# Moving the softmax normalization of attention rows from the writer to the reader: sparse attention and capacity routing on one core

## The chip, the cores and the metric

The kernel runs on one core of one Trainium2 chip. The metric is device time in microseconds (us) of one execution. Before the change, three runs took 1037.57, 1035.76 and 1036.93 us, a median of 1036.93 us. One more execution was recorded by the hardware profiler; its own time was 1035.21 us, and the span from its first to its last instruction is 1033.4 us.

Engines go by the names of the profile: PE multiplies matrices, PEld loads its weights, DVE is the vector engine, ACT the scalar engine, POOL the general-purpose engine (GpSimd), SP issues DMAs. Each engine takes its instructions in the order in which the program lists them.

## The reference

All data are 32-bit floats. Attention runs over 8 batches, 8 heads, 576 positions, 64 elements per head. Its output rows (4608 tokens of 512 elements) go into a mixture of 8 experts in which each expert takes exactly 576 tokens.

```
scores = q @ k^T / 8
scores below (row maximum - tau) are dropped
attn   = exp(scores - max) / sum(exp(scores - max))
x      = attn @ v, the 8 heads of a token side by side   # 4608 x 512
logits = x @ w_gate                                      # 4608 x 8
pairs (token, expert) are taken from the largest logit down;
   an expert that has 576 tokens is full
out[token] = relu(x[token] @ w1[e]) @ w2[e]              # 512 -> 1024 -> 512
```

The division by the sum is a factor for each token and head, so a token of 512 elements has eight factors. It can be applied at any point between `attn @ v` and the expert's first matrix product.

## The kernel before

**Attention.** Four pairs of heads per batch, nine score tiles per pair. PE makes scores, DVE takes the row minimum of the negated scores (`mx`, L74) and applies the threshold (`stt`, L89), ACT takes the exponential (L85), POOL adds tau to the row's extreme (L75), PE transposes the probabilities (L98) and multiplies them by v (L144). The result lies transposed (elements on partitions) and unnormalized in `XT`, one tile per batch. DVE computes reciprocals of the sums into `RD[b]` (token-major, nine columns per pair) and `RD["m",b]` (for the last 64 tokens of a batch).

**Rows.** `xt_unit(b,c)` (L197) turns one chunk of a batch's `XT` back to rows: four PE transposes (L201) into a PSUM bank, then a read of that bank, then a DMA on SP's queue to `xrows` in DRAM (L215). There are five chunks a batch: four of 128 tokens and one of 64 (c = 4), so 40 in all. Two PSUM banks alternate (`bank_v`). For batches 0 and 1 these units run among the attention work, and DVE multiplies by the factors as it reads PSUM (L208, into tile `xr`). For batches 2 to 7 they are kept in `late`; batches 2 and 3 lie in DRAM meanwhile (`xts`). These 30 late units run after the last score tile. There ACT copies PSUM to SBUF and POOL multiplies by the factors (L214, into a free `pp` tile), except for c = 4, where ACT does both in eight pieces of 64 elements (L212).

**Search.** `Router.phase` finds the first expert's tokens: a threshold search of seven levels. A level is a DVE comparison of all best logits with 16 or 32 candidates (`step_cmp`), counts on PE (L403), a DVE copy, flags through PE (L409) and DVE, a broadcast through PE (L419, L424), and a DVE step to the next candidates. Then `pick` chooses the expert, and `pack` (L538) builds the list `idx` of its 576 token numbers. The search for the first expert is interleaved with the 30 late units by the loop at L298: a late unit every `XTY` = 1.05 us of a planned clock, search steps at their planned times. DVE instructions of the router go through the wrapper `Vec`, all shown on line L341.

**Experts.** `moe` keeps jobs (generators) on a planned clock. Each job puts its instructions into the engines' queues and yields a planned wait; `ffn` advances the clock with each matrix product, and the jobs that are due are put in between. So the planned waits set the order of the queues, not the times. An expert r passes through: the search (`R.phase`, waits lengthened by `LATS[r]`), `packing`, then `rows` (L609). `rows` gathers the expert's rows with five indirect DMAs on POOL's queue (L615), waits `GA[r]`, and for each of the five tiles has four PE transposes (L625), an ACT rounding into `xh` (L628), a wait of 0.8, a DVE subtraction into `xl` (the rounding's rest), and a wait of `RW[r]` (0.2, 0.6, 1.0, then 2.0). Two weight jobs split `w1` and `w2` the same way (ACT rounds, DVE subtracts). `ffn` of expert r starts in the plan when its weights and rows are marked done: all five row tiles for r of 2 and more; three tiles (c = 4, 0, 1) for r of 0 and 1, which start with one half of the tokens. While it isn't done, the plan's clock runs on without matrix products. For r = 0 and 1, POOL does most of the subtractions behind relu (L655); for r of 2 and more, DVE does them. `place` runs one search after the other; for r = 0 it waits 2.3 after the packing, closes the expert (`R.close`, five DVE instructions that mark taken tokens and the full expert), waits 1.4 and begins the next search.

Of the kernel before, what the change touches and what calls it, by code (L numbers as in the profile page):

```python
# [9 lines left out]
F32 = mybir.dt.float32  # L10
# [3 lines left out]
AF = mybir.ActivationFunctionType  # L14
ALU = mybir.AluOpType
# [3 lines left out]
S=576; D=64; HS=288; QK=3*HS+2*S  # L19
PPB=8; LTB=1; VTB=5; HOLD=1; CAPV=3.3; RATE=(2.4,2.4); NBO=2; XAC=(4,); NDEF=4; XTB=4; XTY=1.05; XT0=2.0; XRB=2  # L20


def attention(ctx, tc, qk, vl, tau, wgd, xrows, xts, Lg, nb_batches, ident, swap, R, after_first):
# [129 lines left out]
    RD={}  # L153
# [43 lines left out]
    def xt_unit(b,c):  # L197
        ps=bank_v([128,4,128])
        n=128 if c<4 else 64
        for j in range(4):  # L200
            T.transpose(ps[:n,j],XT[b][:,j,c*128:c*128+n],ident)  # L201
        if b<nb_batches-NDEF-NBO: xr=wk.tile([128,512],F32,name="xr",bufs=XRB)
        else: xr=wk.tile([128,2,S],F32,name="pp",bufs=PPB)[:,0,:512]
        def ev():
            src=RD[b][:,:,2*c:2*c+2] if c<4 else RD["m",b][0:64]
            src=src.unsqueeze(3).to_broadcast([n,4,2,64])
            xv=xr[:n].rearrange("p (j h d) -> p j h d",j=4,h=2); pv=ps[:n].rearrange("p j (h d) -> p j h d",h=2)
            if b<nb_batches-NDEF-NBO: V.tensor_tensor(xv,pv,src,op=ALU.mult)  # L208
            elif c in XAC:
                for j in range(4):  # L210
                    for h in range(2):
                        A.activation(xv[:,j,h],pv[:,j,h],AF.Copy,scale=RD[b][:n,j,2*c+h:2*c+h+1] if c<4 else RD["m",b][0:64,j,h:h+1])  # L212
            else:
                A.activation(xv,pv,AF.Copy); G.tensor_tensor(xv,xv,src,op=ALU.mult)  # L214
            nc.sync.dma_start(xrows[b*S+c*128:b*S+c*128+n,:],xr[:n])  # L215
        return ev
# [335 lines left out]

LATS=[0.15,0.05,0.4]+[0.6]*5; FIX=(0.125,0.2)
GA=[7.0,5.5,7.5,9.0]; HALF=1; WARM=[20,4,50]
W1Y=5.0; L2O=(0,4,1,2,3); L2Z=1; HFB=3; RW=[0.2,0.6,1.0,2.0]; LOWP=(0,1); LPF=7; LOWT=1.4; PREPW=1; WLY=(1.0,1.0)

def moe(ctx,tc,R,start,xrows,w1,w2,out,ident):
# [51 lines left out]
    def rows(r,s):  # L609
        while r>0 and ("x",r-1) not in done: yield 0.5  # L610
        order=(4,0,1,2,3) if r<=HALF else range(5)
        for t in order:
            n=128 if t<4 else 64
            x=wk.tile([128,D],F32,name="xg",bufs=5); s["xg",t]=x
            G.indirect_dma_start(out=x[:n],out_offset=None,in_=xrows,in_offset=IOA(ap=s["idx"][:n,t:t+1],axis=0))  # L615
        s["ei2"]=wk.tile([128,1],I32,name="ei2",bufs=2); G.tensor_copy(s["ei2"],s["ei"])
        done.add(("g",r))
        yield GA[min(r,3)]
        while r>0 and ("l1",r-1) not in done: yield 0.5
        s["xh"]=wk.tile([128,4,576],F32R,name="xh"); s["xl"]=wk.tile([128,4,576],F32R,name="xl")  # L620
        for t in order:
            n=128 if t<4 else 64
            ps=pt.tile([128,4,128],F32,name="pt")
            held[0]+=0.5
# [3 lines left out]
            A.activation(xv("xh"),pv,AF.Copy)  # L628
            yield 0.8
            V.tensor_tensor(xv("xl"),pv,xv("xh").bitcast(F32),op=ALU.subtract)  # L630
            done.add(("row",r,t))
# [47 lines left out]
    def place():  # L679
        for r in range(8):  # L680
# [17 lines left out]
            if r==0:  # L698
                yield from packing(r,s)
                yield 2.3; R.close(); yield 1.4  # L700
            else:
                if r<7: R.close()
                jobs.append([clk[0],packing(r,s)])
                yield 0.1
# [57 lines left out]
def build(tc, qk, vl, tau, wgd, cst_d, w1, w2, out, off, nb=8):  # L762
    nc=tc.nc
    with ExitStack() as ctx:
        ctx.enter_context(tc.manual_schedule())
        cp=ctx.enter_context(tc.tile_pool(name="cst",bufs=1))
        dr=ctx.enter_context(tc.tile_pool(name="dr",bufs=1,space=bass.MemoryType.DRAM))
        xrows=dr.tile([8*S,512],F32,name="xrows")
        xts=dr.tile([8,128,4,S],F32,name="xts")
# [28 lines left out]
```

## Time and profile before

| what | value |
|---|---|
| median of 3 runs | 1036.93 us (1035.76 to 1037.57) |
| the profiled execution's own time | 1035.21 us |
| its span | 1033.4 us |
| PE busy | 975.2 us (94%) |
| DVE busy | 777.4 us (75%) |
| ACT busy | 640.0 us (62%) |
| POOL busy | 323.1 us (31%) |
| mean granted clock of PE | 0.982 of full speed |

A share of busy time is a mean over stages with different limits, so the stages are to be read one by one. Attention's score tiles run to about 482 us, the late rows and the first search from there to 537 us, and the experts from 537 us to the end. A group line of the profile gives line, engine, operation, the tile written and the tiles read, shape and count, then busy time in us and the mean of one in ns, then the engine's idle time before these instructions and what ended it. A row of the timeline gives start and duration in us, then the instruction, and in brackets the idle time before it and what ended it.

### The profile page before, as it was taken

The page shows a single profiled execution, that of the slowest core. Times are in us where ns is not written, and L with a number is a line of the kernel's source. Part 1 is how long each engine was busy: PE and PEld are TensorE (multiplying, and loading weights), DVE is VectorE, ACT ScalarE, POOL GpSimd, SP SyncE. Part 2 cuts the span into 40 slices and gives each one's busy share as a digit, 9 for nine tenths or more (in the row PEclk, how much of TensorE's full clock was granted, in tenths as well). Part 3 has the DMA queues.
Part 4 walks back from the last instruction along what each step waited for, and adds up shares of the span by engine and source line. Part 5 has one row for each costly group of instructions (what it writes and reads, how often), then busy time and mean ns, then how long its engine had stood idle before and what let it go on. Part 6 is the DMA issues. An engine that isn't in the chain of part 4 may idle for free. (4 is left out here: it accounts for less than half of the span.)

```text
span 1033.4 us, 24027 instructions
## 1 busy us (share of the span) xinstructions
PE 975.2 (94%) x9104; PEld 709.5 (69%) x9104; DVE 777.4 (75%) x2085; ACT 640.0 (62%) x1221; POOL 323.1 (31%) x485
## 2 busy tenths in 40 slices
PE   6999999999999999998658899999999999999996
PEld 3555555555555555555547779788897978889895
DVE  6999999999999999996777677757585676744230
ACT  5898888888888888886644335444352534445340
POOL 2333333333333343331653445312204031231201
PEclk9999999999999999999878999999999999999998
DMA  6322133233433222302453251504325052363101
GB/s 224 106 67 96 65 138 127 95 138 113 153 107 107 96 72 100 108 2 93 158 206 122 82 169 48 197 28 131 130 83 168 14 185 75 125 229 127 41 11 41
DMA packets 35715, 113.03 MB, mean 109 GB/s; under 512 B 4368, under 2 KB 4752, under 8 KB 35088
## 3 DMA queue, kind: packets, MB, share of 16 engines
q1 hardware_dynamic: 28496, 89.47, 24.5%
q0 software_dynamic: 5888, 18.88, 5.8%
q10 hardware_dynamic: 1216, 3.15, 0.9%
q8 instruction: 72, 1.18, 0.5%
q14 instruction: 43, 0.35, 0.1%
HBM read 89.19 MB, written 21.23 MB: 107 GB/s over the span
## 5 line engine op out<-in xcount | busy, mean ns | idle before, releaser
L75 POOL TENSOR_SCALAR nb<-nb,taub 128x1 f32<-128x1 f32 x288 | 146.8, 510 | 296.6 <-DVE z L74 256.1
L74 DVE TENSOR_SCALAR_CACHE_REDUCE z<-sc 128x576 f32<-128x576 f32 x288 | 206.0, 752 | 34.0 <-PE sc L69 32.5
L85 ACT ACTIVATE pp<-z,nb 128x576 f32<-128x576 f32 x256 | 187.3, 772 | 34.3 <-DVE z L74 32.8
L89 DVE SCALAR_TENSOR_TENSOR pp<-z,nb,pp 128x576 f32<-128x576 f32 x256 | 199.9, 813 | 0.3
L665 PE MATMUL pf<-w2h,H 128*128 128x512 f32 x576 | 196.1, 402 | 1.1 <-DVE H L341 1.1
L69 PE MATMUL sc<-qk 64*128 64x288 f32 (+1 forms) x1280 | 181.3, 428 | 6.0 <-DMA qk<-qk_dram 5.7
L144 PE MATMUL xo<-pt,vt 128*64 128x288 f32 x1024 | 151.9, 418 | 0.7 <-ACT xt L151 0.7
L113 ACT ACTIVATE pt<-tb 128x512 f32<-128x512 f32 x256 | 140.0, 593 | 13.8 <-PE tb L98 11.7
L98 PEld LDWEIGHTS tb<-ident,pp 64*128 64x128 f32 x2304 | 85.7, 139 | 72.7 <-ACT pt L113 16.8
L665 PE MATMUL pf<-w2l,H 128*128 128x512 f32 x320 | 128.2, 401 | 0.0
L672 POOL DMA_INDIRECT out_dram<-y,idx x40 | 42.0, 1050 | 266.8 <-ACT y L668 170.0
L665 PEld LDWEIGHTS pf<-w2h,H 128*128 128x128 f32 x576 | 106.4, 189 | 19.9 <-DVE H L341 1.5
L98 PE MATMUL tb<-ident,pp 64*128 64x64 f32 x2304 | 108.8, 230 | 11.4 <-ACT pt L113 6.2
L69 PEld LDWEIGHTS sc<-qk 64*128 64x128 f32 (+1 forms) x1280 | 94.3, 179 | 35.9 <-DVE pp L89 9.2
L645 PE MATMUL pf<-xh,w1h 128*128 128x288 f32 x512 | 113.3, 300 | 1.2 <-ACT xh L628 1.2
L645 PE MATMUL pf<-xh,w1l 128*128 128x288 f32 x512 | 113.6, 300 | 0.0
L645 PE MATMUL pf<-xl,w1h 128*128 128x288 f32 x512 | 112.8, 299 | 0.0
L651 ACT ACTIVATE hf<-pf 128x576 f32<-128x576 f32 x64 | 41.7, 652 | 105.0 <-PE pf L645 94.0
L144 PEld LDWEIGHTS xo<-pt,vt 128*64 128x64 f32 x1024 | 62.5, 136 | 63.6 <-issue 26.5
L668 ACT ACTIVATE y<-pf 128x512 f32<-128x512 f32 x40 | 23.9, 598 | 115.9 <-PE pf L665 105.1
L645 PEld LDWEIGHTS pf<-xh,w1h 128*128 128x128 f32 x512 | 82.8, 189 | 3.8 <-ACT xh L628 1.7
L645 PEld LDWEIGHTS pf<-xl,w1h 128*128 128x128 f32 x512 | 82.4, 189 | 0.2 <-DVE xl L341 0.2
(170 smaller groups left out, 1355.5 us busy)
## 6 DMA issues: line engine op xcount, KB each, us to landing
qk<-qk_dram SPq DMA_DIRECT2D x31, 1008.0 KB, 4.9
w2s<-w_dram SPq DMA_DIRECT2D x32, 512.0 KB, 5.9
w1s<-w_dram SPq DMA_DIRECT2D x28, 512.0 KB, 5.8
vt<-vl_dram SPq DMA_DIRECT2D x32, 320.0 KB, 5.4
xrows<-pp SPq DMA_DIRECT2D x24, 256.0 KB, 2.0
xts<-xt SPq DMA_DIRECT2D x2, 1152.0 KB, 5.3
pt<-xts SPq DMA_DIRECT2D x2, 1152.0 KB, 6.8
xrows<-xr SPq DMA_DIRECT2D x8, 256.0 KB, 2.0
```

What stands on the lines that cost most here:

```text
L69: T.matmul(sc[o,f,:HS], kd["q",h][r,c], kd[k,h][r,:],start=True,stop=True)
L74: V.tensor_scalar(z,SC.pop(t)[:,:,:HS],-0.125,None,op0=ALU.mult,op1=ALU.min,accum_out=nb[:,0:1])
L75: G.tensor_scalar(nb[:,1:2],nb[:,0:1],taub[:,0:1],None,op0=ALU.add)
L85: A.activation(pview(t),ZB[t].rearrange("p a b -> p (a b)"),AF.Exp,bias=NBI[t][:,0:1],scale=-1.0)
L89: V.scalar_tensor_tensor(pv,ZB.pop(t).rearrange("p a b -> p (a b)"),NBI[t][:,1:2],pv,op0=ALU.is_le,op1=ALU.mult,accum_out=den_of(p)[:,p%4, ...
L98: g=slice(64*r,64*r+64); T.transpose(o[:,r],x[g],ident[g,g])
L113: A.activation(PT[p][:,i%2,:,(i//2)*128:(i//2+1)*128].rearrange("p k (r q) -> p r k q",r=2),tb,AF.Copy)
L144: T.matmul(xo[64*h:64*h+64,:HS],v[:,u,64*h:64*h+64],PT[p][:,h,u,q],start=(u==0),stop=False,skip_group_check=True)
L645: T.matmul(ps[:,h,:HS],s[w][:,k,f*128:(f+1)*128],s[x][:,k,h*HS:(h+1)*HS], start=(k==0 and j==0),stop=(k==3 and j==2))
L651: A.activation(hf,ps[:,:,:HS],AF.Relu)
L665: T.matmul(ps[:,0,:],H[:,f,c:c+128],s[w][:,f],start=(f==0 and j==0),stop=e)
L672: G.indirect_dma_start(out=out,out_offset=IOA(ap=s["idx"][:n,t:t+1],axis=0),in_=y[:n],in_offset=None)
```

## The change

Rows go to DRAM unnormalized, with their eight factors beside them: a row of `xrows` has 520 elements (2080 bytes) instead of 512 (2048 bytes). The gathered tiles `xg` have the same width, and DVE multiplies each head's 64 elements by its factor before the transposes, for all 40 tiles.

In `xt_unit`, DVE (batches 0 and 1) and ACT (the rest) only copy PSUM to SBUF; the factors are copied by POOL (batches 0 and 1) or ACT (the rest). POOL's multiplications over 512 elements and ACT's eight-piece multiplications for c = 4 are gone. In `rows`, expert 0's multiplications stand between the tiles' other steps; for later experts all five stand ahead of the first transpose, with a planned wait of `SCY` = 1.2 after each. Three planned quantities change: `LATS[1]` from 0.05 to 0.15, `GA` from 7.0, 5.5, 7.5, 9.0 to 6.0, 6.5, 8.0, 9.0, and the start of the second search, which was 3.7 after expert 0's list and now comes when expert 0's third row tile has been put into the queues.

```diff
-PPB=8; LTB=1; VTB=5; HOLD=1; CAPV=3.3; RATE=(2.4,2.4); NBO=2; XAC=(4,); NDEF=4; ...
+PPB=8; LTB=1; VTB=5; HOLD=1; CAPV=3.3; XW=520; RATE=(2.4,2.4); NBO=2; NDEF=4; ...
...
-        if b<nb_batches-NDEF-NBO: xr=wk.tile([128,512],F32,name="xr",bufs=XRB)
-        else: xr=wk.tile([128,2,S],F32,name="pp",bufs=PPB)[:,0,:512]
+        early=b<nb_batches-NDEF-NBO
+        if early: xr=wk.tile([128,XW],F32,name="xr",bufs=XRB)
+        else: xr=wk.tile([128,2,S],F32,name="pp",bufs=PPB)[:,0,:XW]
         def ev():
             src=RD[b][:,:,2*c:2*c+2] if c<4 else RD["m",b][0:64]
-            src=src.unsqueeze(3).to_broadcast([n,4,2,64])
-            xv=xr[:n].rearrange("p (j h d) -> p j h d",j=4,h=2); pv=ps[:n].rearrange("p j (h d) -> p j h d",h=2)
-            if b<nb_batches-NDEF-NBO: V.tensor_tensor(xv,pv,src,op=ALU.mult)
-            elif c in XAC:
-                for j in range(4):
-                    for h in range(2):
-                        A.activation(xv[:,j,h],pv[:,j,h],AF.Copy,scale=RD[b][:n,j,2*c+h:2*c+h+1] if c<4 else RD["m",b][0:64,j,h:h+1])
+            fv=xr[:n,512:XW].rearrange("p (j h) -> p j h",j=4); xv=xr[:n,:512].rearrange("p (j d) -> p j d",j=4)
+            if early:
+                V.tensor_copy(xv,ps[:n]); G.tensor_scalar(fv,src,1.0,0.0,op0=ALU.mult,op1=ALU.add)
             else:
-                A.activation(xv,pv,AF.Copy); G.tensor_tensor(xv,xv,src,op=ALU.mult)
+                A.activation(xv,ps[:n],AF.Copy); A.activation(fv,src,AF.Copy)
...
-LATS=[0.15,0.05,0.4]+[0.6]*5; FIX=(0.125,0.2)
-GA=[7.0,5.5,7.5,9.0]; HALF=1; WARM=[20,4,50]
+SCY=1.2; LATS=[0.15,0.15,0.4]+[0.6]*5; FIX=(0.125,0.2)
+GA=[6.0,6.5,8.0,9.0]; HALF=1; WARM=[20,4,50]
...
-            x=wk.tile([128,D],F32,name="xg",bufs=5); s["xg",t]=x
+            x=wk.tile([128,XW],F32,name="xg",bufs=5); s["xg",t]=x
...
+        def scale(t):
+            n=128 if t<4 else 64
+            v=s["xg",t][:n,:D].rearrange("p (h d) -> p h d",h=8)
+            V.tensor_tensor(v,v,s["xg",t][:n,D:XW].unsqueeze(2).to_broadcast([n,8,64]),op=ALU.mult)
         yield GA[min(r,3)]
+        if r>0:
+            for t in order: scale(t); yield SCY
         while r>0 and ("l1",r-1) not in done: yield 0.5
...
         for t in order:
             n=128 if t<4 else 64
+            if r==0 and t==order[0]: scale(t)
...
             yield 0.8
+            if r==0 and t!=order[-1]: scale(order[order.index(t)+1])
             V.tensor_tensor(xv("xl"),pv,xv("xh").bitcast(F32),op=ALU.subtract)
...
-                yield 2.3; R.close(); yield 1.4
+                yield 2.3; R.close(); yield 0.1
+                while ("row",0,1) not in done: yield 0.1
...
-        xrows=dr.tile([8*S,512],F32,name="xrows")
+        xrows=dr.tile([8*S,XW],F32,name="xrows")
```

More of the change, by code (lines that the diff above doesn't have):

```diff
@@ L19 @@
 S=576; D=64; HS=288; QK=3*HS+2*S
-PPB=8; LTB=1; VTB=5; HOLD=1; CAPV=3.3; RATE=(2.4,2.4); NBO=2; XAC=(4,); NDEF=4; XTB=4; XTY=1.05; XT0=2.0; XRB=2
+PPB=8; LTB=1; VTB=5; HOLD=1; CAPV=3.3; XW=520; RATE=(2.4,2.4); NBO=2; NDEF=4; XTB=4; XTY=1.05; XT0=2.0; XRB=2
 def attention(ctx, tc, qk, vl, tau, wgd, xrows, xts, Lg, nb_batches, ident, swap, R, after_first):
```

## The prediction

> **What bounds the kernel now.** I read the table of stretches first (columns: stretch and its length, busy us and instruction count of PE, PEld, DVE, ACT and POOL, granted PE clock, DMA share, GB/s):
>
> ```profile
> 300.00:400.00 100.00, 98.88 (x1154) 57.44 (x1154) 94.01 (x271) 87.71 (x163) 35.39 (x70) 1.00 0.27 96
> 491.00:531.00 40.00, 24.14 (x221) 18.93 (x222) 28.32 (x61) 23.89 (x72) 27.60 (x24) 0.79 0.51 178
> 531.00:548.00 17.00, 10.15 (x113) 8.62 (x112) 14.10 (x29) 5.81 (x7) 6.72 (x6) 0.70 0.58 193
> 620.00:680.00 60.00, 59.22 (x458) 50.72 (x456) 43.55 (x103) 24.96 (x50) 26.30 (x26) 1.00 0.32 110
> ```
>
> Attention and the experts are bound by PE (98.9% and 98.7% busy). Between them lie 57 us, 491 to 548, in which PE is busy for 34 us at a clock of 0.7 to 0.8. That is the seam: the late rows, the first search and the first gather. Next the waits of PE from 491 to 531 (line that waits, line waited for, total us, times, longest), and the search's DVE groups there:
>
> ```profile
> PE sc L403 <- DVE cmp L341: 9.1, 6, 2.8
> PE xo L201 <- ACT pp L212: 2.1, 2, 1.2
> ```
>
> ```profile
> L341 DVE TENSOR_TENSOR cmp<-b,E 128x1152 bf16<-128x1152 f32 x4 | 7.6, 1904 | 0.1
> L341 DVE TENSOR_TENSOR cmp<-b,E 128x576 bf16<-128x576 f32 x2 | 2.3, 1152 | 0.1
> L341 DVE TENSOR_SCALAR E<-cst,sm 128x34 f32<-128x34 f32 x2 | 2.1, 1054 | 0.1
> ...
> L341 DVE TENSOR_TENSOR oh<-oh,ge 128x288 bf16<-128x288 bf16 x1 | 1.3, 1295 | 0.0
> ...
> L341 DVE TENSOR_TENSOR q<-Lg,b 128x64 bf16<-128x64 f32 x1 | 1.1, 1119 | 0.0
> ...
> L341 DVE SCALAR_TENSOR_TENSOR E<-cst,sm,E 128x34 f32<-128x34 f32 x1 | 1.0, 985 | 0.0
> L341 DVE SCALAR_TENSOR_TENSOR sm<-sm 128x1 f32<-128x1 f32 x1 | 1.0, 969 | 0.0
> ```
>
> The longest wait is for the comparisons: the seam is bound by the search on DVE. And its instructions are far too long. The same operations after 545 us:
>
> ```profile
> L341 DVE TENSOR_TENSOR cmp<-b,E 128x576 bf16<-128x576 f32 x12 | 9.1, 755 | 0.3
> L341 DVE TENSOR_TENSOR cmp<-b,cst 128x1152 bf16<-128x1152 f32 x6 | 8.1, 1352 | 0.0
> ...
> L341 DVE TENSOR_TENSOR oh<-oh,ge 128x288 bf16<-128x288 bf16 x7 | 4.3, 613 | 0.2
> ...
> L341 DVE TENSOR_SCALAR E<-cst,sm 128x34 f32<-128x34 f32 x12 | 3.4, 281 | 0.4
> ...
> L341 DVE TENSOR_TENSOR q<-Lg,b 128x288 bf16<-128x288 f32 x6 | 2.8, 458 | 0.2
> ...
> L341 DVE SCALAR_TENSOR_TENSOR E<-cst,sm,E 128x34 f32<-128x34 f32 x6 | 1.6, 266 | 0.2
> ...
> L341 DVE SCALAR_TENSOR_TENSOR sm<-sm 128x1 f32<-128x1 f32 x6 | 1.0, 160 | 0.2
> ```
>
> A one-element instruction takes 0.97 us in the seam and 0.16 us later. What differs is POOL's multiplications (480 to 540 us), each about as long as the excess:
>
> ```profile
> L214 POOL TENSOR_TENSOR pp<-pp,rd 128x512 f32<-128x512 f32 x24 | 27.6, 1174 | 10.3 <-ACT pp L214 10.2
> ```
>
> So POOL's 27.6 us, off the path by itself, lengthens the DVE work that is on it. [...]
>
> **The change, part by part.** *Late rows.* The 24 POOL multiplications go. The excess of the seven groups: 4 x (1.904-1.352) + 2 x (1.152-0.755) + 2 x (1.054-0.281) + (1.295-0.613) + (1.119-0.458) + (0.985-0.266) + (0.969-0.160) = 2.2+0.8+1.5+0.7+0.7+0.7+0.8 = 7.4 us. ACT's side (480 to 548 us):
>
> ```profile
> L214 ACT ACTIVATE pp<-xo 128x512 f32<-128x512 f32 x24 | 14.2, 598 | 12.7 <-PE xo L201 9.4 <-issue 1.7 <-PE sc L419 0.5
> L212 ACT ACTIVATE pp<-xo,rm 64x64 f32<-64x64 f32 x48 | 10.2, 308 | 2.5 <-POOL pp L214 1.5 <-PE xo L201 0.6 <-PE sc L419 0.5
> L127 ACT ACTIVATE pl<-tb 64x64 f32<-64x64 f32 x1 | 0.2, 219 | 0.0
> ```
>
> The 48 pieces become six copies of 0.6, and 30 factor copies are added, priced by the nearest small ACT copy, 0.22. ACT then needs 30 x 0.82 = 24.6 us, against 14.2+10.2 = 24.4 before: no gain in sum, but evenly spread, and PE's 2.1 us of waits for the pieces end. Together 7.4+2.1 = 9.5 us, which I take. Lower bound 5: two PSUM banks alternate, and the late rows last 36 us now (timeline, 491 to 527); in 26.5 us, ACT's 24.6 nearly fill them; half the gain may stick there. Upper bound 12, since smaller lengthened groups are not counted. SP's row DMAs only get earlier.
>
> *Early rows, batches 0 and 1.* Ten DVE multiplications become copies of the same size, and POOL gets ten small instructions. On POOL's queue the `nb` steps stand behind them, which the thresholds on DVE need.
>
> ```profile
> L208 DVE TENSOR_TENSOR xr<-xo,rd 128x512 f32<-128x512 f32 x4 | 2.7, 668 | 0.0
> L75 POOL TENSOR_SCALAR nb<-nb,taub 128x1 f32<-128x1 f32 x288 | 146.8, 510 | 296.6 <-DVE z L74 256.1
> ```
>
> Ten at 0.51 us are 5 us on a POOL that is 35% busy beside a PE at 98.9%, so 0. Without that cover it costs 5 us; with no multiplication to read a second input DVE could give back part of 6.7 us. I allow -1 to +2.
>
> *Wider rows.* 1.6% more bytes; on the median 3.7 us from issue to landing of a gather that is below 0.1 us, and only expert 0's is on the path. Were a row moved in two pieces, twice 3.7 us bounds it from above.
>
> ```profile
> xg<-xrows,idx POOLq DMA_INDIRECT x40, 3.7
> ```
>
> *Expert 0's start.* From the timeline (list ready, `close`, next search, transposes, last `xh`):
>
> ```profile
> 536.60 0.16 DVE L341 SCALAR_TENSOR_TENSOR idx<-cps,ih 128x5 int32<-128x5 f32 x1
> ...
> 539.62 1.94 POOL L615 DMA_INDIRECT xg<-xrows,idx  x1 [0.30 <-issue]
> 541.87 0.95 POOL L615 DMA_INDIRECT xg<-xrows,idx  x1 [0.30 <-issue]
> ...
> 543.42 0.44 DVE L341 TENSOR_REDUCE b<-Lg 128x36 f32<-128x288 f32 x1
> 544.02 1.12 PE L625 MATMUL pt<-ident,xg 128*128 128x128 f32 x4 [1.82 <-DMA xg<-xrows,idx]
> ...
> 546.06 1.12 PE L625 MATMUL pt<-ident,xg 128*128 128x128 f32 x4 [0.93 <-DVE xl L341]
> ...
> 551.15 0.60 ACT L628 ACTIVATE xh<-pt 128x512 fp32r<-128x512 f32 x1 [1.19 <-PE pt L625]
> ```
>
> ```profile
> L341 DVE TENSOR_TENSOR xl<-pt,xh 128x512 fp32r<-128x512 f32 x32 | 22.0, 689 | 21.8 <-ACT xh L628 21.6
> ```
>
> A multiplication of 128x512 is the size of an `xl` subtraction, 0.69 us. The first two wait for their gathers, so 0.7 us of each adds before its transposes. In return the second search's preparation, which now delays `xl` by 0.9 us at 546, moves behind the third tile; it then stands ahead of the last tiles' multiplications (five instructions of about the 0.44 of the row, 2.1 us). Sum: 0.7+0.7-0.9 for the first tiles, then 1 of the 2.1 exposed: +1.5. Bounds 0 and 3.7. [...]
>
> *Later experts.* 35 multiplications, 3.4 us of DVE for each expert, on a DVE busy 43.6 of 60 us. PE covers them. Without that cover: 3.4 us an expert. What is not covered is lateness of order. The second search began 3.7 after expert 0's list in the plan; now it waits for the third tile, 6.0+1.0+1.0+0.8 = 8.8, while expert 0's products may start at 8.8 instead of 9.8: 6.1 later against them. `LATS[1]` adds 0.1 at 23 waits, 2.3. `rows` adds 5 x 1.2 = 6.0. From expert 3 on, that is 14.4 of planned lateness, and the room before is (last transposes, start of the next expert's products):
>
> ```profile
> 735.03 0.46 PE L625 MATMUL pt<-ident,xg 64*128 64x64 f32 x4
> 740.36 0.42 PE L645 MATMUL pf<-xh,w1h 128*128 128x288 f32 x2
> ```
>
> ```profile
> 859.64 0.46 PE L625 MATMUL pt<-ident,xg 64*128 64x64 f32 x4
> ...
> 860.72 0.54 PE L645 MATMUL pf<-xh,w1h 128*128 128x288 f32 x2 [0.51 <-ACT xh L628]
> ```
>
> The plan holds the products back until 0.8+2.0 after the last transposes. At expert 3 there is 5.3-2.8 = 2.5 of room, at expert 5 none: 1.1-2.8 = -1.7. So all 14.4 must be made good by experts 1 to 5: the plan lets search and rows run on without products between them. What that costs PE, expert 5 shows: 1.7 of planned lateness left PE idle for 0.51 us, 0.30 per unit, since the rows were long there. 14.4 x 0.30 = 4.3 us. Bounds: 0, if DVE and ACT are always ahead; 14.4 x 43.6/60 = 10.5, if DVE has to work off what it does in such a stretch.
>
> Sum: -9.5 + 0 + 1.5 + 4.3 = -3.7 us. Against the profiled execution's 1035.2 (span 1033.4 and 1.8 around it) that is 1031.5; this execution lies 1.7 below the median of the runs, so against 1036.9 it is 1033.2, the forecast.
>
> **The rivals.** *Slower: the order's lateness is paid in full and grows.* Place: between one expert's last product and the next one's first. The planner counts each multiplication on its DVE clock too (0.73), 3.7 an expert, and a search waits for that clock; if half goes into each of the five searches for experts 2 to 6, lateness grows from 14.4 to 23.6. At 0.73 us per unit that is 17.2 us, against -9.5+1.5 = -8.0 without it: +9.2, 1046.1. It decides from 8.0+2.1 = 10.1 us of idle PE, 0.43 per unit. For it: experts 3 to 5 have no room. Against: 0.30 where it can be read. *Nothing to measure: ACT and the two banks pace the late rows,* gain 5: -5+1.5+4.3 = +0.8, 1037.7. For it: 24.6 us on ACT. Against: PE's longest wait is 9.1 us for DVE. *Faster still: lateness is free,* since the gathered rows lie ready: -8.0, 1028.9. For it: PE idle 0.8 us of 60 in 620 to 680. *It doesn't do what it says:* DVE's length has another cause (the low clock stage, bank waits), and only PE's 2.1 us come back: -2.1+1.5+4.3 = +3.7, 1040.6. Against: of the two comparisons of 128x576 in the seam, with a mean of 1.152, one took as long as later, between two of POOL's multiplications:
>
> ```profile
> 501.46 0.76 DVE L341 TENSOR_TENSOR cmp<-b,E 128x576 bf16<-128x576 f32 x1
> ```
>
> **How the numbers follow.** Forecast 0.44, lateness free 0.22, paced by ACT 0.15, lateness in full 0.15, not what it says 0.04. Two executions of this kernel differ by up to 1.8 us, so 0.2% (2.1 us) is about what can be told from no change. Faster: 0.40 of the forecast's 0.44, the 0.22 and 0.02 of the paced case, 0.64. Slower: 0.15 and 0.03, 0.18. The rest, 0.18, is no change. The range: from the upper bound 12 with nothing lost later, 1024.9, rounded to 1025, up to 1041, which takes in the fourth case and stops short of the slow one's 1046; about 0.1 lies on either side.
>
> **What would show it.** DVE's comparisons of 128x1152 in the seam at 1.35 us, no POOL multiplication there, and the list about 9.5 us earlier than 536.76. Expert 0's last `xh` some 16.5 us after the list, now 551.75-536.76 = 15.0. PE idle between experts, with transposes and search matrix products alone between L665 and the next L645, 4 us in sum. The forecast is wrong if the list comes less than 6 us earlier (ACT paces), if PE's idle time after 560 us grows by over 8 us, or if attention before 480 us gets longer.

## The result, and the profile after

The changed kernel takes 1050.51 us (median of 4 runs, 1050.39 to 1052.4), the kernel before 1036.88 beside it. The ratio is 1.014 with a 95% interval of 1.0127 to 1.0152: 13.6 us slower. The forecast was 1033.2, 3.7 us faster; the time lies outside its range and has the other sign. The profiled execution of the changed kernel took 1052.4 us, its span 1050.6.

The seam did what it was meant to. DVE's groups by shape, 480 to 545 us of the changed kernel (the columns as before):

```profile
L338 DVE TENSOR_TENSOR cmp<-b,E 128x1152 bf16<-128x1152 f32 x4 | 5.4, 1359 | 0.1
L338 DVE TENSOR_TENSOR cmp<-b,E 128x576 bf16<-128x576 f32 x2 | 1.5, 758 | 0.1
L338 DVE TENSOR_SCALAR E<-cst,sm 128x34 f32<-128x34 f32 x2 | 0.5, 274 | 0.1
L338 DVE TENSOR_TENSOR oh<-oh,ge 128x288 bf16<-128x288 bf16 x1 | 0.5, 458 | 0.0
```

The comparisons of 128x1152 went from 1904 to 1359 ns, the 34-element step from 1054 to 274: the excess is gone. The list of expert 0, its start, its last `xh`, and the list of the seventh expert, in the timeline of the changed kernel:

```profile
525.77 0.17 DVE L338 SCALAR_TENSOR_TENSOR idx<-cps,ih 128x5 int32<-128x5 f32 x1
...
537.32 0.61 PE L651 MATMUL pf<-xh,w1h 128*128 128x288 f32 x1 [0.69 <-ACT xh L633]
...
540.63 0.60 ACT L633 ACTIVATE xh<-pt 128x512 fp32r<-128x512 f32 x1 [1.22 <-PE pt L630]
...
906.96 0.17 DVE L338 SCALAR_TENSOR_TENSOR idx<-cps,ih 128x5 int32<-128x5 f32 x1
```

In the kernel before, the seventh list stands here:

```profile
897.48 0.17 DVE L341 SCALAR_TENSOR_TENSOR idx<-cps,ih 128x5 int32<-128x5 f32 x1
```

The first list comes 10.8 us earlier than before (525.77 against 536.60), the seventh 9.5 us later. So 20.3 us are lost between two lists that both kernels build by the same search. Where an expert's first product starts (L645 before, L651 after), from the two timelines, in us:

| expert | 0 | 1 | 2 | 3 | 4 | 5 | 6 | 7 | end |
|---|---|---|---|---|---|---|---|---|---|
| before | 547.9 | 619.2 | 681.0 | 740.4 | 800.6 | 860.7 | 919.8 | 973.2 | 1033.4 |
| after | 537.3 | 610.3 | 681.0 | 748.0 | 811.4 | 873.5 | 934.4 | 990.1 | 1050.6 |
| after less before | -10.6 | -8.9 | 0.0 | 7.6 | 10.8 | 12.8 | 14.6 | 16.9 | 17.2 |

The gain of 10.6 us at expert 0 is used up by expert 2, and 27.8 us are lost by the end of the span. (The span grew by 17.2 us, the medians by 13.6: the profiled execution before was a quick one of its kernel, the one after a slow one of its own.) Expert 0 even gains up to its second products (570.9 against 584.6, 13.7 ahead); from there to expert 1's first, its second and expert 2's first products 4.8, 5.4 and 3.5 us go, and 7.6 more to expert 3. There PE has gaps that the kernel before doesn't have. The table of stretches, kernel before and then kernel after (the columns are those of the prediction):

```profile
605.00:619.00 14.00, 13.66 (x89) 10.23 (x88) 9.78 (x27) 4.54 (x9) 4.78 (x6) 1.00 0.67 228
```

```profile
600.00:604.00 4.00, 1.42 (x19) 0.91 (x18) 4.00 (x6) 1.63 (x3) 3.52 (x4) 1.00 0.56 144
604.00:608.00 4.00, 1.12 (x5) 0.71 (x4) 3.93 (x13) 1.88 (x4) 0.48 (x1) 0.56 0.97 374
608.00:612.00 4.00, 2.36 (x8) 1.67 (x8) 3.88 (x9) 1.15 (x3) 1.05 (x2) 0.50 0.60 223
612.00:616.00 4.00, 3.73 (x27) 3.34 (x26) 0.82 (x3) 1.23 (x3) 0.80 (x1) 0.66 0.19 70
616.00:620.00 4.00, 3.66 (x28) 3.42 (x28) 2.06 (x5) 2.17 (x4) 0.00 (x0) 1.00 0.00 0
...
740.00:800.00 60.00, 56.18 (x424) 49.33 (x422) 43.87 (x116) 25.43 (x50) 9.34 (x10) 0.94 0.33 109
```

The same middle stretch in the kernel before, and then the whole from expert 0's first product to the end, before and after:

```profile
740.00:800.00 60.00, 59.51 (x451) 51.44 (x450) 41.91 (x110) 25.54 (x50) 12.65 (x13) 1.00 0.36 115
```

```profile
547.90:1033.40 485.50, 469.26 (x3364) 409.57 (x3364) 289.06 (x723) 198.42 (x389) 123.25 (x118) 0.99 0.31 105
```

```profile
537.30:1050.60 513.30, 483.50 (x3364) 422.12 (x3364) 310.52 (x765) 197.90 (x389) 118.62 (x118) 0.96 0.29 99
```

PE has the same 3364 matrix instructions in both. Of the 27.8 us, 13.6 are more idle time of PE (29.8 against 16.2), and 14.2 are more busy time for the same instructions, at a mean granted clock of 0.96 instead of 0.99.

Ahead of expert 1's products PE is busy for 4.9 of the 12 us from 600 to 612, while DVE is busy for 11.8. The granted clock falls to 0.5 and stands at 1.00 again in the row from 616. The same place in the timeline of PE:

```profile
599.96 0.39 PE L671 MATMUL pf<-w2h,H 128*128 128x512 f32 x1
...
602.27 0.29 PE L406 MATMUL rps<-cn,e 128*32 128x8 f32 x4 [1.50 <-DVE cn L338]
...
605.62 0.16 PE L421 MATMUL rps<-fla,onesb 128*128 128x1 bf16 x1 [2.67 <-DVE jka L338]
...
608.51 1.09 PE L630 MATMUL pt<-ident,xg 128*128 128x128 f32 x4 [1.77 <-issue]
610.28 0.61 PE L651 MATMUL pf<-xh,w1h 128*128 128x288 f32 x1 [0.69 <-ACT xh L633]
611.98 0.44 PE L651 MATMUL pf<-xh,w1h 128*128 128x288 f32 x1
...
617.11 0.29 PE L651 MATMUL pf<-xh,w1h 128*128 128x288 f32 x1
```

Ten us pass between the last product of expert 0 and the first of expert 1. In them PE has only the next search's matrix products and the row transposes, in the order of the plan. A product takes 0.44 us behind the gap and 0.29 when the clock is back at 1.00, so the time of such a gap shows twice: once as itself, and once in the products behind it.

### The profile page after: what moved, and what is told of

It is laid out like the page before. It is cut to its first block, busy times and chain, and to the rows that moved or that the text cites. A ratio compares the mean times of both kernels' runs of the same rounds, so it can differ in the third digit from the quotient of the medians.

```text
span 1050.6 us, 24017 instructions
## 1 busy us (share of the span) xinstructions
PE 988.3 (94%) x9104; PEld 721.5 (69%) x9104; DVE 787.4 (75%) x2125; ACT 635.5 (60%) x1209; POOL 295.6 (28%) x471
## 5 line engine op out<-in xcount | busy, mean ns | idle before, releaser
L671 PE MATMUL pf<-w2h,H 128*128 128x512 f32 x576 | 193.8, 400 | 0.4 <-DVE H L338 0.4
L671 PE MATMUL pf<-w2l,H 128*128 128x512 f32 x320 | 128.2, 401 | 0.0
L651 PE MATMUL pf<-xh,w1h 128*128 128x288 f32 x512 | 118.5, 311 | 2.8 <-ACT xh L633 2.8
L671 PEld LDWEIGHTS pf<-w2h,H 128*128 128x128 f32 x576 | 107.0, 188 | 20.2 <-DVE H L338 0.8
L651 PE MATMUL pf<-xl,w1h 128*128 128x288 f32 x512 | 118.0, 310 | 1.6 <-DVE xl L338 1.5
L651 PE MATMUL pf<-xh,w1l 128*128 128x288 f32 x512 | 116.8, 308 | 0.0
L144 PEld LDWEIGHTS xo<-pt,vt 128*64 128x64 f32 x1024 | 62.6, 136 | 63.6 <-issue 26.5
L651 PEld LDWEIGHTS pf<-xh,w1h 128*128 128x128 f32 x512 | 86.9, 198 | 4.5 <-ACT xh L633 4.0
L651 PEld LDWEIGHTS pf<-xl,w1h 128*128 128x128 f32 x512 | 86.3, 197 | 3.2 <-DVE xl L338 3.2
```

What stands on the lines that cost most here:

```text
L144: T.matmul(xo[64*h:64*h+64,:HS],v[:,u,64*h:64*h+64],PT[p][:,h,u,q],start=(u==0),stop=False,skip_group_check=True)
L651: T.matmul(ps[:,h,:HS],s[w][:,k,f*128:(f+1)*128],s[x][:,k,h*HS:(h+1)*HS], start=(k==0 and j==0),stop=(k==3 and j==2))
L671: T.matmul(ps[:,0,:],H[:,f,c:c+128],s[w][:,f],start=(f==0 and j==0),stop=e)
```

## The experiments

Most runs differ from the changed kernel in a few lines of its planner, and each time stands beside that of the kernel before from the same chip. "Counted" means that an instruction goes through the wrapper `Vec` (`V.`), which adds its length to the planner's DVE clock `V.free`; called on DVE directly (`nc.vector`) the same instruction runs on the chip and the planner doesn't know of it. A search step's planned wait ends `LATS[r]` after that clock. In the kernel's text only the waits of the search and of the packing read `V.free`, so the count can act through them alone.

### The writer alone and the plan alone

`seam_only` is the changed writer with the planned waits of before and without the multiplications (the output lacks the normalization). `plan_only` is the kernel before with the planned waits of the change alone:

```diff
 # plan_only, against the kernel before
-LATS=[0.15,0.05,0.4]+[0.6]*5; FIX=(0.125,0.2)
-GA=[7.0,5.5,7.5,9.0]; HALF=1; WARM=[20,4,50]
+LATS=[0.15,0.15,0.4]+[0.6]*5; FIX=(0.125,0.2)
+GA=[6.0,6.5,8.0,9.0]; HALF=1; WARM=[20,4,50]
         yield GA[min(r,3)]
+        if r>0:
+            for t in order: yield 1.2
...
-                yield 2.3; R.close(); yield 1.4
+                yield 2.3; R.close(); yield 0.1
+                while ("row",0,1) not in done: yield 0.1
```

> The change's writer alone (unnormalized rows with their factors, no POOL multiplication), with the planned waits of before. The multiplication of the gathered rows is left out, so the output lacks the normalization. Both theories: the seam gives its whole gain, 10 to 14 us, so 1023 to 1027 us, and nothing is lost later. If the time is above 1032 us, the loss after expert 0's start has to do with the writer or the wider rows, and both theories fall.

> The kernel before with the change's planned waits alone: the second search starts when expert 0's third row tile is queued, LATS[1] is 0.15, GA is 6.0, 6.5, 8.0, 9.0, and five waits of 1.2 stand ahead of each later expert's transposes, with no multiplication behind them. Theory A (lateness of order: the planned waits put search and row tiles behind the previous expert's last product, and PE starves between experts): slower by what the changed kernel lost after expert 0's start, 27 us (its expert 0 started 10.5 us earlier and its end came 17.2 us later), so some 1055 to 1067 us. Theory B (the 40 multiplications themselves, 27.6 us of DVE work, slow the searches): 1035 to 1040 us, no change.

`seam_only` took 1026.17 us against 1036.55, a ratio of 0.9905 (0.9887 to 0.9923): -10.4 us. `plan_only` took 1047.13, 1.0124 (1.0077 to 1.0171): +10.6 us, without one instruction more or less on any engine. So the gain in the seam is real and of the size that was worked out. The planned waits alone, which change nothing but the order of the queues, cost 10.6 us, a figure between the ranges of the two theories: they are part of the 24.0 us lost behind the seam (13.6 and 10.4), and not all of it.

### Multiplications elsewhere, and the gap filled

`scale_inline` has all multiplications, counted, the waits of before, and in place of the five waits of 1.2 each multiplication one tile ahead of its transposes. `warm_gap` is the changed kernel with idle products of PE put into the planned gaps, meant to hold the clock up:

```diff
 # scale_inline (its other lines go back to the waits of before)
-            for t in order: scale(t); yield SCY
+        if r>0: scale(order[0]); yield 0.8
...
-            if r==0 and t!=order[-1]: scale(order[order.index(t)+1])
+            if t!=order[-1]: scale(order[order.index(t)+1])
 # warm_gap
             now+=0.25; run(now)
+            if r>0: R.warm(2)
```

> The change with all 40 multiplications, but with the planned waits of before: the second search starts 3.7 after expert 0's list, LATS[1] and GA as before, and a later expert's multiplications stand between its tiles' other steps (0.8 of planned wait for the first one, none for the others). Theory A: 1024 to 1031 us, the seam's gain without the loss. Theory B: 1043 to 1052 us.

> The changed kernel with two idle-time matrix products (into a corner of the search's PSUM bank that nobody reads) for every 0.25 of planned clock in which the plan waits for rows of expert 1 or later. Theory A says that 14 us of the loss lie in the gaps and some 13 us in the slow clock that follows each gap (matrix products of 0.44 instead of 0.29 us at the start of expert 1). If the slow clock is a cost of its own, 1037 to 1043 us; if it is not, or the gaps are too short to be filled, 1049 to 1053 us.

`scale_inline` took 1061.78, 1.0248 (1.023 to 1.0266): slower than the changed kernel, though the waits of 1.2 are gone, and above the ranges of both theories. `warm_gap` took 1050.94, 1.0144 (1.0126 to 1.0162), as the changed kernel. At expert 1's start the clock recovers earlier there (0.97 from 612 to 616 us, 0.66 in the changed kernel):

```profile
604.00:608.00 4.00, 2.80 (x25) 2.49 (x25) 2.35 (x6) 0.63 (x1) 0.61 (x1) 0.67 1.04 404
608.00:612.00 4.00, 3.64 (x29) 3.51 (x29) 3.53 (x11) 1.50 (x3) 0.32 (x1) 0.50 0.52 187
612.00:616.00 4.00, 3.43 (x36) 2.98 (x35) 2.28 (x5) 1.72 (x3) 0.98 (x1) 0.97 0.17 66
```

The stages of the first products (from the first product on L651 to the first on L671) are 11.1 us shorter in sum than in the changed kernel, and the stages behind them with their gaps 10.2 us longer. So part of the time shows in the low clock, but something else sets the end.

### Counted or not, executed or not

Three runs take the multiplications apart: `after_noscale` leaves them out and keeps the five waits (no normalization); `count_only` leaves them out but adds their length to the planner's clock (no normalization either); `scale_uncounted` executes them and doesn't count them. `lats_short` keeps all and shortens the search's waits.

```diff
 # after_noscale (the other calls of scale are removed too)
-            for t in order: scale(t); yield SCY
+            for t in order: yield SCY
 # count_only
-            V.tensor_tensor(v,v,s["xg",t][:n,D:XW]...,op=ALU.mult)
+            V.free=max(V.free,V.now)+V.fix+0.512/0.96
 # scale_uncounted
-            V.tensor_tensor(v,v,s["xg",t][:n,D:XW]...,op=ALU.mult)
+            nc.vector.tensor_tensor(v,v,s["xg",t][:n,D:XW]...,op=ALU.mult)
 # lats_short
-LATS=[0.15,0.15,0.4]+[0.6]*5
+LATS=[0.15,0.15,0.2]+[0.3]*5
```

> The changed kernel with all its planned waits, but without the 40 multiplications, neither in DVE's queue nor on the planner's DVE clock; the output lacks the normalization. The seam's gain (-10.4 in the run with the writer alone) and the planned waits' cost (+10.6 in the run with the waits alone) should add to about zero if they are independent: 1034 to 1040 us. Then some 13 us of the loss belong to the multiplications. If planned waits are the whole loss (theory A), it stays at 1047 to 1052 us.

> As the run without multiplications, but each is still counted on the planner's DVE clock (0.2 + 0.533), so that search steps are put into the queues as late as in the changed kernel; the output lacks the normalization. Theory C (the loss comes through the planner's clock: between the first and the seventh list the searches take 381 us instead of 361): 1046 to 1052 us. Theory B (the multiplications' own time on DVE): 1034 to 1040 us, like the run without them.

> The changed kernel with its multiplications in DVE's queue, but not counted on the planner's DVE clock. Theory C: 1033 to 1041 us, since the searches are ordered as without them. Theory B: 1046 to 1056 us, since DVE falls behind an order that leaves it no room.

> The changed kernel with the planned waits of the searches for experts 2 and later cut in half (LATS 0.2 and 0.3 for 0.4 and 0.6). About 23 waits a search make each of them 5 to 7 us shorter in the plan. If the order's pace of search is what holds PE back (theories A and C): 1034 to 1043 us. If DVE's real work is (theory B): 1049 us or more, since the same work is only asked for earlier and PE waits for it at the head of its queue.

| kernel | us (before: 1037.34) | ratio, 95% interval |
|---|---|---|
| `after_noscale` | 1036.56 | 0.9989 (0.9977 to 1.0001) |
| `count_only` | 1050.82 | 1.0123 (1.0103 to 1.0142) |
| `scale_uncounted` | 1040.76 | 1.0033 (1.0021 to 1.0044) |
| `lats_short` | 1038.22 | 1.0005 (0.9995 to 1.0015) |

Counting instructions that don't exist costs 14.3 us (`count_only` less `after_noscale`), and makes the kernel as slow as the change. Executing them without the count costs 4.2. In the changed kernel the count costs 9.7 (1050.5 less 1040.8). `after_noscale` came out in its first range, the other three in those of theory C. The first and the seventh list, first in `count_only`, then in `after_noscale`:

```profile
525.02 0.17 DVE L338 SCALAR_TENSOR_TENSOR idx<-cps,ih 128x5 int32<-128x5 f32 x1
...
905.63 0.17 DVE L338 SCALAR_TENSOR_TENSOR idx<-cps,ih 128x5 int32<-128x5 f32 x1 [0.21 <-DVE ih L338]
```

```profile
524.76 0.17 DVE L338 SCALAR_TENSOR_TENSOR idx<-cps,ih 128x5 int32<-128x5 f32 x1
...
892.17 0.16 DVE L338 SCALAR_TENSOR_TENSOR idx<-cps,ih 128x5 int32<-128x5 f32 x1
```

The six list intervals last 380.6 us with the count, 63.4 each, and 367.4 without, 61.2 each. In the kernel before they last 360.9, 60.1 each, about what the starts of its experts 2 to 5 in the table above are apart (59.4, 60.2, 60.1): there products and searches keep pace. With the count the lists come 63.4 us apart, and the starts of experts 2 to 5 in `count_only` 68.2, 63.3 and 62.9. `count_only` also shows that the full DVE in the gap isn't what holds it: from 600 to 612 us DVE is busy for 6.9 us in place of 11.8, and the gap between expert 0's last product and expert 1's first is 9.9 us long as in the changed kernel (598.44 to 608.30 in the timeline of `count_only`).

```profile
600.00:612.00 12.00, 6.14 (x36) 4.85 (x37) 6.86 (x20) 5.25 (x10) 3.20 (x4) 0.61 0.64 231
```

```profile
600.00:612.00 12.00, 4.89 (x32) 3.29 (x30) 11.81 (x25) 4.66 (x9) 5.06 (x6) 0.69 0.71 247
```

(The first row is of `count_only`, the second of the changed kernel.)

### The five waits, and shorter waits

`noscale_scy0` is `after_noscale` without the five waits of 1.2. The other three execute the multiplications uncounted: `free_short` with the `LATS` of `lats_short`; `free_short_scy` with `SCY` 0.6 as well; `free_shorter` with `LATS` 0.05, 0.1 and 0.2 (experts 1, 2 and 3 to 7) and `SCY` 0.9.

> The run without multiplications (1036.6 us, output lacks the normalization), and without the five planned waits of 1.2 ahead of a later expert's transposes; the later start of the second search, LATS[1] and GA stay as in the changed kernel. Of the 14.4 of planned lateness, 6.0 go. By theory A in proportion: 10.4 x 6.0/14.4 = 4.3 us come back, 1031 to 1034 us. If only the search's place counts and not the waits behind the gather: 1035 to 1038 us.

> The changed kernel with both effective edits at once: multiplications not counted on the planner's DVE clock, and LATS 0.2 and 0.3 for experts 2 and later. Theory C: the two act on the same lateness (each alone 1038 to 1041 us), so less than the sum of 9.8 and 12.3 us comes back; what is left are experts 1's and 3's starts: 1029 to 1036 us, faster than before. Theory B (DVE has no time for the searches that early): 1038 us or more.

> As the run before in this list, with the planned wait after each multiplication 0.6 instead of 1.2: 3.0 less lateness of the row tiles, at the price of multiplications that may wait on DVE for their gathers. Theory C: 1 to 2.5 us below the run with 1.2. If DVE waits for the gathers: equal or slower.

> Multiplications not counted, LATS 0.05 for the second search and 0.1 and 0.2 for the later ones, planned wait 0.9. Theory C: expert 1's start, which still costs most (its two stages are 11 us longer than before in the run with shorter waits), gains some 2 us from the second search: 1026 to 1034 us. Theory B: 1038 us or more.

| kernel | us (before: 1037.28) | ratio, 95% interval |
|---|---|---|
| `noscale_scy0` | 1021.97 | 0.9845 (0.9828 to 0.9861) |
| `free_short` | 1038.76 | 1.0013 (1.0004 to 1.0023) |
| `free_short_scy` | 1037.91 | 0.9991 (0.9968 to 1.0015) |
| `free_shorter` | 1042.69 | 1.0044 (1.0031 to 1.0056) |

Against the kernel before of its own batch, `noscale_scy0` gains 15.3 us and `after_noscale` 0.8, so the five waits cost 14.5; its 1022.0 lies below both of the expected ranges. And `noscale_scy0`, which keeps the later start of the second search, the longer `LATS[1]` and the new `GA`, gains 4.9 more than `seam_only`, which has none of them: in this order the three together cost nothing. `free_short` and `free_shorter` came out where theory B put them, at 1038 us or more, and `free_short_scy` gained 0.9 on the run with 1.2, within its interval. Not counting and shortening each give 10 to 12 us in the changed kernel, but both together give no more than the better of them, and still shorter waits cost 4 us. So it isn't a matter of ever shorter waits. Which waits would be best in that order, these runs don't tell.

### The waits away, the multiplications kept

`scy0` is the changed kernel with `SCY` = 0, `scy0_free` the same uncounted. `inline_free` is uncounted and puts the first multiplication behind `GA` with a wait of 0.8, and each further one just ahead of the transposes of the tile before it; it leaves nothing of the computation out. `inline_counted` is the same, counted, and `inline_counted_lats` has the `LATS` of `lats_short` beside that.

```diff
 # inline_counted; inline_free calls nc.vector.tensor_tensor in scale as well
         if r>0:
-            for t in order: scale(t); yield SCY
+            scale(order[0]); yield 0.8
...
             if r==0 and t==order[0]: scale(t)
+            if r>0 and t!=order[-1]: scale(order[list(order).index(t)+1])
```

> The changed kernel with one number changed: the planned wait after each multiplication is 0 instead of 1.2. Without multiplications this took 14.6 us off (1036.6 to 1022.0). Theory C (two separate costs, the planned waits 14.6 us and the count on the planner's DVE clock 14 us): 1034 to 1038 us. If the five multiplications, now in one block, make DVE wait for the gathers and PE wait for DVE: 1042 us or more.

> The same, and the multiplications are not counted on the planner's DVE clock. Theory C: 1040.8 - 14.6, some 1024 to 1030 us, faster than before by about as much as the seam gives. If DVE's real work now binds (theory B, which only an order without slack can show): 1033 us or more, with PE waiting for multiplications at the head of its queue.

> Not counted, no planned waits of 1.2, and a later expert's multiplications spread: the first after GA with a wait of 0.8, each other one just ahead of the transposes of the tile before it. Each then comes after its gather has landed. If waiting for gathers is what costs in the block: 1 to 5 us below it, 1022 to 1030 us. If the PE waits for DVE anyway: 1033 us or more, as when they were spread and counted (1061.8).

> The tight order of inline_free (the first multiplication after GA and 0.8, each next one just ahead of the transposes of the tile before it, no waits of 1.2), but every multiplication counted on the planner's DVE clock again (0.73 units each, 3.7 an expert). Theory A, the count and the five planned waits are two costs that add: the count costs the 10 to 14 us that it cost beside the waits, so 1039 to 1043. Theory B, the planned waits of 1.2 gave the counted clock time to run out, so without them a search that follows sees all 3.7 units: the count costs what it did with SCY 0 (1060.8 against 1034.0, 26.8), so about 1056.

> As inline_counted, with LATS 0.2 and 0.3 in place of 0.4 and 0.6 for experts 2 to 7, which takes 0.3 from each wait of a search. If the count acts only by making the planned search longer than an expert's products, the shorter waits give back most of it: 12 us as they did in the changed kernel (1050.5 to 1038.2), or more. If it acts through the place of the instructions on DVE, they give back little: under 5 us.

| kernel | us | before beside it | ratio, 95% interval |
|---|---|---|---|
| `scy0` | 1060.84 | 1036.8 | 1.0234 (1.0217 to 1.0251) |
| `scy0_free` | 1033.98 | 1036.8 | 0.9977 (0.9968 to 0.9987) |
| `inline_free` | 1029.24 | 1036.8 | 0.9924 (0.9907 to 0.994) |
| `inline_counted` | 1051.32 | 1037.15 | 1.0134 (1.0117 to 1.0151) |
| `inline_counted_lats` | 1045.07 | 1037.15 | 1.0076 (1.0058 to 1.0093) |

`scy0` and `scy0_free` came out in the second of their ranges (1042 us or more, 1033 or more); in `scy0` the count alone is 26.9 us of that. `inline_free` came out in its first. Against `noscale_scy0`, each beside its own kernel before, the executed multiplications cost 12.5 us in one block (`scy0_free`, -2.8 against -15.3) and 7.7 spread (`inline_free`, -7.6): in an order without slack DVE's work itself costs time, with no count.

What the count costs depends on the order that it falls into: 9.7 us with the five waits, 26.9 with the waits at zero, 22.1 with one multiplication a tile. Taking the waits away while the count stays makes things worse by 10.3 us (`scy0` against the changed kernel), while without the count it gains 6.8. The two prices therefore don't add, and `inline_counted` with 1051.3 lies between the 1043 of theory A and the 1056 of theory B.

The pair `inline_free` and `inline_counted` shows the mechanism most cleanly. The first and the seventh list of each:

```profile
525.74 0.17 DVE L338 SCALAR_TENSOR_TENSOR idx<-cps,ih 128x5 int32<-128x5 f32 x1
...
890.83 0.17 DVE L338 SCALAR_TENSOR_TENSOR idx<-cps,ih 128x5 int32<-128x5 f32 x1
```

```profile
525.57 0.17 DVE L338 SCALAR_TENSOR_TENSOR idx<-cps,ih 128x5 int32<-128x5 f32 x1
...
913.16 0.16 DVE L338 SCALAR_TENSOR_TENSOR idx<-cps,ih 128x5 int32<-128x5 f32 x1
```

Both issue the same instructions to every engine. The seventh list comes 22.3 us later where the planner counts, and the span is 21.7 us longer (1049.9 against 1028.2): the whole loss is there by the seventh list. The lists are late before the products are: the third comes 9.5 us later (659.05 against 649.60), though expert 1's second products, ahead of it, start only 1.1 later (640.04 against 638.93), and expert 2's first products then start 6.4 later (678.18 against 671.83).

`inline_counted_lats` gave back 6.3 us, between the 12 and the under 5 that were expected. The seventh list is back at 902.46, 10.7 us earlier, but the span only 6.2 shorter. The difference arises early: expert 3's list comes 10.2 us earlier (717.88 against 728.12) and its first product only 6.0 (742.68 against 748.68). Behind 560 us PE's waits for the multiplied rows stand second there, with 4.2 us:

```profile
PE rps L406 <- DVE cn L338: 5.6, 5, 1.6
PE pt L630 <- DVE xg L338: 4.2, 6, 2.0
```

`inline_free` beats both kernels, by 7.6 and by 21 us. Its stretches in the middle of the experts hold the clock at 1.00:

```profile
620.00:680.00 60.00, 57.86 (x437) 49.76 (x434) 43.58 (x107) 23.79 (x47) 21.10 (x22) 1.00 0.34 113
...
740.00:800.00 60.00, 59.26 (x445) 50.79 (x444) 44.20 (x114) 24.25 (x48) 12.34 (x12) 1.00 0.35 113
```

## Why the prediction was wrong

**Late rows, -9.5: right.** `seam_only` gave -10.4 at the end and the list came 10.8 us earlier, between the -9.5 taken and the bound of -12. The comparisons came out at 1.36 us, with 1.35 forecast. POOL has no multiplication in the seam now, and the excess is gone, by 0.55 us a comparison and 0.78 a 34-element step. PE's wait for the comparisons fell from 9.1 us to this:

```profile
PE sc L400 <- DVE cmp L338: 3.8, 6, 1.0
```

Two readings were off. One of the seven groups was compared with a larger one (`q` of 64 elements in the seam, of 288 later); it now takes 225 ns, so the sum of 7.4 was 0.2 too small. And POOL's 1174 ns were called about as long as the excess, which was 400 to 810 ns for an instruction. ACT and the two banks did not set the pace, so that rival falls, and the one by which the change doesn't do what it says falls too. That POOL's instructions were the cause is not shown by this alone: the rows agree with it, but no run takes away POOL's multiplications and nothing else.

**Early rows, 0, and wider rows, under 0.1: right.** The first late row unit starts at 491.62 us, 0.6 later than before. DVE's ten copies of the early rows take 680 ns at the median, and its eight multiplications of 128x512 took 684, so of the 6.7 us next to nothing came back. A gather's median time to landing is 3.7 us, as before:

```profile
xg<-xrows,idx POOLq DMA_INDIRECT x40, 3.7
```

**Expert 0's start, +1.5: about right.** The last `xh` ends at 541.23, 15.3 us after the end of its list, against 15.0 before: +0.3, within the bounds of 0 and 3.7. Its four parts weren't measured singly.

**Later experts, +4.3: this is the step that failed.** It measured 27.8 us in the two traces, and 24.0 by the medians (13.6 and the 10.4 of the seam); its upper bound of 10.5 was wrong as well. Three things in it were wrong.

First, its list of what is late. It priced the second search, `LATS[1]` and the five waits, 14.4 planned units, and "35 multiplications ... PE covers them" at nothing. Read in one order along the runs, each taken against the kernel before of its own batch: the seam -10.4 (`seam_only`), the second search with `LATS[1]` and `GA` -4.9 (`noscale_scy0` at -15.3), the five waits +14.5 (`after_noscale` at -0.8), the count +14.3 (`count_only` at 13.5), the executed multiplications +0.2 (the change at 13.6). So 8.4 of the 14.4 units cost nothing in this order (with them `GA`'s longer waits for experts 1 and 2, which the sum left out). The two large prices are about equal, the five waits and the count, and the count wasn't in the sum at all; it stood in the rival alone. In another order (`scale_uncounted` ahead of the count) the multiplications cost 4.2 and the count 9.7. The forecast that DVE's 3.4 us an expert lie beside PE's work about holds as long as the order is loose. In a tight one they cost 7.7, with a planned wait of 0.8 beside them (`inline_free` against `noscale_scy0`).

Second, its rate. The 0.30 us per planned unit came from one place, a single late start at expert 5 behind a run of long products. The five waits measure 14.5 us for 6.0 planned units, 2.4 per unit. The prediction counted them once, but all seven later experts have them, 42 units in all, and over those the price is 0.35 per unit, near the rate that was read. From `after_noscale` and `noscale_scy0` the delay is paid at the starts of experts 2, 3, 4 and 7 (4.0, 5.6, 1.9 and 2.2 us more each time, 1.2 or less at the others). Of the 14.1 us by which these two traces differ from expert 0's start to the end, 8.5 lie in the stages of the first products of experts 1 to 7, which follow the gaps.

Third, the assumption that products set the pace. With 59 to 60 us for an expert on PE and 60.1 between lists, the search had next to no room (in the plan of the kernel before, the products of experts 4 to 6 wait 3.5 units for their rows already), and the count of 3.7 units an expert falls on the searches' planned waits: lists 63.4 us apart instead of 61.2, 64.6 (`inline_counted`) instead of 60.8. The prediction looked for room on the engines (DVE busy 43.6 of 60 us) and not on the planner's clock.

**The rivals.** "The order's lateness is paid in full and grows" named the place, the sign and the count on the planner's clock; its price of 17.2 us was too low against 27.8, with 0.73 us per unit and half of the count. "Lateness is free" falls for the whole; of its parts it holds for the second search and `LATS[1]`. What the prediction set as its sign of failure, over 8 us more idle PE behind 560 us, came (28.8 us against 15.5), together with a lower clock that it hadn't foreseen.

**The plan's own clock shows most of it.** The planner knows nothing of the chip, so its clock follows from the kernel's text alone, from the waits that the jobs yield. Worked out in this way, the plan of the kernel before runs 443.4 units from expert 0's first product to expert 7's last. The table gives by how much each plan is longer, and by how much its profiled execution is longer than the 485.5 us of the kernel before, from expert 0's first product to the end:

| kernel | plan, units | trace, us |
|---|---|---|
| `noscale_scy0` | +0.3 | -0.6 |
| `after_noscale` | +10.5 | +13.5 |
| the changed kernel | +21.9 | +27.8 |
| `scale_uncounted` | +10.5 | +15.3 |
| `inline_counted` | +22.9 | +27.2 |
| `inline_free` | +3.5 | +5.6 |
| `scy0` | +26.8 | +35.5 |
| `scy0_free` | +0.3 | +9.4 |
| `lats_short` | +7.7 | +13.9 |
| `inline_counted_lats` | +5.5 | +20.9 |
| `free_shorter` | -2.9 | +19.7 |

In the plan the count costs 11.4 units beside the five waits, 19.4 with one multiplication a tile and 26.5 with the waits at zero. Measured were 9.7 (14.3 without the multiplications), 22.1 and 26.9 us, so that its price changes with the order lies in the plan. How far the chip follows a plan, the plan can't tell: the trace is up to 9.2 us longer in the rows down to `lats_short`, but 15.4 and 22.6 us in the last two.

**Open** is what sets the time in these last two. That DVE doesn't keep up with such an order is what theory B says, and the 4.2 us of waits for the multiplied rows agree, but they are a part only.

## What to carry to other kernels

Where a hand-written planner orders the queues by a clock of its own, an instruction has two prices, one on its engine and one in the planner's account, and the second can be the larger: the same instructions gave 1029 us uncounted and 1051 counted. Before a planned wait is added, compare the period of the longest planned chain (here a search, 60.1 us) with the period of the bounding engine (59 to 60), since a chain without room can pay an added unit again in every pass. The plan's own clock can be worked out ahead of any run: here it was 21.9 units longer, where the prediction put 4.3 us. A gain ahead of a pipeline is best measured by itself, with the pipeline's plan as it was, and the plan then tuned to the new start; it was 10.4 us here and stood all along under a loss of 24.

## What the hardware showed unexpectedly

**The clock takes the gap's cost again.** In a stretch in which PE had 4.9 us of work in 12 (600 to 612 us) the granted clock fell to 0.5, and it was at 0.66 still in 612 to 616, with PE busy for 3.73 of 4 us. In stretches of 1 us it is 1.00 up to 604 us, 0.74 from 604 to 605 and 0.50 from 605 to 614; so it fell inside PE's longest wait there, which lasts 2.67 us, behind one of 1.50. Filling the gaps with idle products raised the mean clock from 0.978, the median of the changed kernel's runs, to 0.987 and gained nothing (1050.9 against 1050.5): the stages of the first products became 11.1 us shorter and the others 10.2 longer.

**The long instructions moved along with the multiplications.** One of expert 1's multiplications ran beside POOL's addition for expert 0's output and took 2.14 us, the next one 0.67. First DVE's rows, then POOL's, in the timeline of the changed kernel:

```profile
602.14 2.14 DVE L338 TENSOR_TENSOR xg<-xg 128x512 f32<-128x512 f32 x1
...
604.81 0.67 DVE L338 TENSOR_TENSOR xg<-xg 128x512 f32<-128x512 f32 x1
```

```profile
602.45 1.27 POOL L681 TENSOR_TENSOR y<-y,z 64x512 f32<-64x512 f32 x1
```

In the changed kernel one more multiplication took as long, 2.09 us at 736.21, beside the addition at 736.45. In `inline_free` there are five, of 1.74 to 2.11 us (at 599.93, 664.89, 725.28, 789.35 and 908.88), and each runs beside one of POOL's additions of 1.29 to 1.54 us. One pair, DVE's row and POOL's:

```profile
725.28 1.88 DVE L619 TENSOR_TENSOR xg<-xg 128x512 f32<-128x512 f32 x1
```

```profile
725.30 1.30 POOL L681 TENSOR_TENSOR y<-y,z 64x512 f32<-64x512 f32 x1
```

So in these two kernels a multiplication moved from POOL to DVE was long where it ran beside an addition of POOL's (1.74 to 2.14 us), and took 0.67 to 0.69 elsewhere. These are coincidences in time; no run moved the additions away.
